# A planner without floors under the latest times of its early pieces

## The chip, the cores and the metric

The kernel runs on one core of a Trainium2 chip. The metric is the device time of one execution in microseconds (us). A core has TensorE (PE in the profile, with its weight loads as PEld), VectorE (DVE), ScalarE (ACT), GpSimd (POOL), and DMA queues; this kernel issues all its transfers from SyncE (SP).

## What is computed

An attention between two sets of rows, in both directions, gives 2304 tokens of 512 numbers (4 batches of 512 and of 32 rows); two MLPs follow, one behind the other. Everything is float32.

```python
# x: 4 x 8 x 512 x 64, state: 4 x 8 x 32 x 64
a  = softmax(x @ state.T / 8);   xread = a @ state
a2 = softmax(state @ x.T / 8);   sread = a2 @ x
x  = concatenate([xread, sread])           # as 2304 tokens x 512

h = x @ w_in                               # 512 -> 2048
x = (h * tanh(softplus(h))) @ w_out        # 2048 -> 512

xn = x / rms(x) * rms_g
g, val = xn @ w_gate, xn @ w_val           # 512 -> 1536
out = (g * sigmoid(g) * val) @ w_out2      # 1536 -> 512
```

## The kernel before

**Precision.** A matmul of the MLPs is made of three f16 matmuls: each operand is a high and a low f16 part, scaled by a power of two. The parts have to be made on the chip. Inputs arrive as 64-bit floats in this kernel, so a block of weights goes through a chain of steps: a load of two halves of 1 MB each into a staging region (L543), the rebuilding of a 32-bit float from its words (high words L470 or L468, sign L562, low word L567 or L569, joined at L578), a sum of squares (L599 on ACT) that a matmul with ones adds over the partitions (L481 on PE), a power-of-two scale from it (L489 to L497 on DVE, products of scales at L507), and then the split: the high part (L468 on ACT or L472 on DVE) and the low part (L612, DVE only).

**Pieces.** `attention(b)` is the attention of batch b: loads of x (L709), transposes on PE (L714, L723), scores (L737), the softmax over 32 columns on DVE and ACT (L777 to L800), PE's reads of state (L755) with the high part (L468) and the low part (L763) of the result written into the tile `slot` of the batch, and the second direction (`second`, L803 to L838). The state is loaded once, at L674. `plain(w, u)` loads and splits block u of the first MLP's weights; `wi` is w_in, `wo` is w_out, four blocks each. `group(gi, c, us, ...)` is the first MLP for batch c and the weight blocks us: pieces of 12 matmuls of 128x512 in the first layer (L918), the activation on ACT (L929), its high part (L468) and its low part g (L933, DVE), and pieces of 6 matmuls in the second layer (L955), summed in PSUM and copied out at the end of a group (L972). `keep(w, u, k, after)` prepares a block of the second MLP's weights (`wg` gate, `wv` value, `w2` out) in one of two staging regions (`psm` for k = 0, `attm` for k = 1), forms the sums of a product scheme with seven instead of eight block products, splits them, and stores the result to DRAM (L1367, `kept_...`), from where it is loaded again when the second MLP (`gated`) needs it.

**Who sets the order.** No line of the kernel gives the order of the engines' instructions. Each of these pieces registers steps with `op()`: what a step costs on each engine that could do it, what it reads and writes, and for PE's main matmuls a wanted time `at`. The class `Plan` then makes a plan for all engines. `chains()` goes back from the wanted and due times and gives each step a latest time: the steps of DVE and ACT behind it are counted at 5.5 times their cost (`SPARE`). `forward()` walks through time and, whenever an engine is free, gives it the ready step with the smallest latest time (a step that DVE could leave to ACT counts 4 us later there). `backward()` derives new latest times from the plan that was found, and the next round goes forward with those. There are 10 rounds, and the plan with the earliest end is kept. The instructions are then issued in that order, and on the chip semaphores hold each one until its inputs are there. The planner's times are a model; what runs together on the chip is decided by the semaphores.

**Floors.** `op()` also notes a floor, when one is set:

```python
o.floor = None if self.floor is None else self.floor()       # L72
...
if o.floor is not None:                                      # L156, in chains()
    late[o] = max(late[o], o.floor)
```

A step with a floor does not get a latest time below it from its chain of needs; it is then taken later than its chain alone would have it, and steps without a floor go first. Floors enter only into the latest times of the first round; the later rounds start from the plan of that round. T0, the wanted time of the first piece of the first MLP, is 22. Before the change attention 1 and wo block 0 have a floor of 12 (T0 - 10), the blocks 1, 2 and 3 of wi and wo have 22, 62 and 102, attention 2 has 102 and attention 3 has 142. Attention 0 and wi block 0 have none. The prepared blocks of `keep` (122 and more, 222 and more) and the steps of `gated` have floors of their own.

Of the kernel before, what the change touches and what calls it, by code (L numbers as in the profile page):

```python
# [318 lines left out]
def attn_moe_moe_kernel(  # L319
# [23 lines left out]
    P = Plan(nc)  # L343
# [271 lines left out]
    def plain(w, u, m, at, xexp, pool="raw", after=()):  # L615

        def dst(k):
            return m(at + 256 + 512 * k, 512).rearrange("p (a f) -> p a f", a=2)

        def dn(k):  # L620
            return m.names(at + 256 + 512 * k, 512)

        fetch(w, u, dst, dn, pool, after)
        s = norms([(m(at + 256 + 1024 * i, 1024).rearrange("p (a n) -> p a n", a=2), [*dn(2 * i), *dn(2 * i + 1)])
                   for i in range(2)], (w, u), xexp, f"{w}{u}", 2)
        for k in range(4):
            split(m, at, k, s, ((w, u), "s"), f"{w}{u}")
# [314 lines left out]
    def flush():  # L942
        if pending:
            l2(*pending.pop(0))
# [453 lines left out]
    with tc.manual_schedule():  # L1398
# [7 lines left out]
        state_scale()  # L1406
        attention(0)
        plain("wi", 0, *home["wi", 0], XEXP)
        P.floor = lambda: T0 + -10
        attention(1)  # L1410
        P.floor = lambda: T0 + -10
        plain("wo", 0, *home["wo", 0], XEXP)
        P.floor = None
        for u in range(1, U1):
            P.floor = (lambda v: lambda: T0 + v)([0, 40, 80][u - 1])
            plain("wi", u, *home["wi", u], XEXP)
            plain("wo", u, *home["wo", u], XEXP)
        P.floor = None
        bar = op({"X": 0.01}, lambda e: None, w=["early"], after=list(early_raw), name="early")
        every = list(range(U1))  # L1420
        group(0, 0, [0], None, 2)
# [2 lines left out]
        group(3, 1, [1], 3, 3)  # L1424
        group(4, 0, [2, 3], 2, 0)
        flush()
        P.floor = lambda: T0 + 80
        attention(2, clock[0] + DUE2)
        P.floor = None
        group(5, 1, [2, 3], 3, 1)  # L1430
        flush()
        P.floor = lambda: T0 + 120
        attention(3, clock[0] + DUE3)
        P.floor = None
        sread_scale(clock[0] + DUE3)
        done = op({"X": 0.01}, lambda e: None, r=held, after=list(att_ops), name="release")
        for w, u, k in (("wg", 0, 0), ("wv", 0, 0), ("wg", 1, 0), ("wv", 1, 1), ("wg", 2, 0), ("wv", 2, 1),
# [24 lines left out]
T0 = 22.0  # L1462
# [33 lines left out]
```

## Time and profile before

| | before |
|---|---|
| median of 3 runs | 799.59 us (795.63 to 801.95) |
| the profiled execution, its own time | 798.37 us |
| its span | 796.6 us |
| PE busy | 767.1 us (96%) |
| PEld (weight loads) busy | 523.8 us (66%) |
| DVE busy | 634.7 us (80%) |
| ACT busy | 445.2 us (56%) |
| mean granted clock of PE, of full speed | 0.977 |

The span runs from the first to the last recorded instruction of the profiled execution; its own time is 1.8 us longer. Times inside the span count from its start. The granted clock reads 1.00 at 2.4 GHz and 0.50 at 1.2 GHz. A line such as L918 is the line of the kernel that issued the instruction, and "out<-in" are the names of the tiles, so `slot<-a,page,slot` reads a PSUM bank `a`, a scalar in a `page` and the tile `slot`, and writes `slot`. `p` and `a` are PSUM banks, `w` and `w2m` hold the first MLP's weights, `psm` and `attm` are staging regions, `tt` is scratch, `g` holds split activations. "[3.17 <-ACT junk L599]" is idle time of the engine just before the instruction, and the instruction whose end released it.

### The profile page before, as it was taken

Reading aid. Unit: us, or ns where it says so; the run is one execution under the profiler, and the core shown is the slowest. Engines: PE = TensorE matmul, PEld = TensorE weight load, DVE = VectorE, ACT = ScalarE, POOL = GpSimd, SP = SyncE. Lnnn points to the kernel's source line nnn. Section 1 sums busy time; section 2 is a strip of 40 time slices with the busy share of each in tenths; the row PEclk is TensorE's granted clock in tenths of the full one; section 3 lists DMA queues with packets and bytes.
Section 4 is the critical chain, followed back from the end, with each engine's and each line's share of the span. In section 5 each row is a group of like instructions: output and inputs, shape, how many; then the busy total and the mean of one; then the engine's idle time right before and its main releaser. Section 6 shows DMA issues by size and latency. Waiting matters only on the chain.

```text
span 796.6 us, 14334 instructions
## 1 busy us (share of the span) xinstructions
PE 767.1 (96%) x5882; PEld 523.8 (66%) x5882; DVE 634.7 (80%) x1303; ACT 445.2 (56%) x812; POOL 0.7 (0%) x6
## 2 busy tenths in 40 slices
PE   6699999999999989999999999999999999999997
PEld 4344444444444434774457778888888889999996
DVE  3999999997997788899589679758984999566560
ACT  4999997666857577867475353425530744123220
POOL 0000000000000000000000000000000000000000
PEclk9599999999999989999999999999999999999999
DMA  8554643205041734523545964357434745275001
GB/s 208 181 144 168 216 156 106 50 5 204 9 158 53 245 125 199 173 107 124 210 156 205 388 227 150 121 187 278 178 117 170 276 167 186 93 284 204 16 2 67
DMA packets 36950, 125.71 MB, mean 158 GB/s; under 512 B 20116, under 2 KB 20116, under 8 KB 30740
## 3 DMA queue, kind: packets, MB, share of 16 engines
q1 hardware_dynamic: 36884, 124.79, 44.1%
q8 instruction: 46, 0.75, 0.4%
q14 instruction: 20, 0.16, 0.1%
HBM read 101.45 MB, written 23.33 MB: 157 GB/s over the span
## 4 chain that ended last, share of the span: by engine, by line
PE 57%; DVE 26%; ACT 9%; DMA 5%; issue 2%; SPq 1%; DVEq 0%; ACTq 0%
PE p L1103 27%; PE a L1187 13%; PE a L955 7%; PE p L918 5%; DVE g L933 3%; DVE psm L612 2%; PE p L1263 2%; ACT junk L599 2%; DMA kept_wg<-psm 2%; DVE sxm L562 2%; ACT sxm L567 1%; DVE w2m L612 1%; DVE page L507 1%; DMA kept_wv<-attm 1%; ACT psm L468 1%
## 5 line engine op out<-in xcount | busy, mean ns | idle before, releaser
L918 PE MATMUL p<-slot,w 128*128 128x512 f16 (+1 forms) x960 | 189.6, 353 | 0.4 <-ACT tt L468 0.4
L955 PE MATMUL a<-g,w2m 128*128 128x512 f16 (+1 forms) x960 | 187.2, 347 | 0.0
L918 PEld LDWEIGHTS <-w 128*128 128x128 f16 x960 | 87.3, 100 | 92.5 <-issue 6.8
L955 PEld LDWEIGHTS <-w2m 128*128 128x128 f16 x960 | 85.7, 99 | 88.3 <-issue 4.6
L1103 PEld LDWEIGHTS <-w 128*128 128x128 f16 x1344 | 131.4, 98 | 17.5 <-issue 0.3
L1115 DVE TENSOR_TENSOR tt<-p,tt 128x512 f32<-128x512 f32 x120 | 82.2, 686 | 43.8 <-PE p L1103 43.1
L1103 PE MATMUL p<-slot,w 128*128 128x256 f16 x768 | 92.6, 273 | 0.0
L1103 PEld LDWEIGHTS <-attm 128*128 128x128 f16 x672 | 65.7, 98 | 9.5 <-issue 1.0
L1187 PE MATMUL a<-attm,w2m 128*128 128x256 f16 x576 | 65.7, 273 | 0.0
L1187 PEld LDWEIGHTS <-w2m 128*128 128x128 f16 x576 | 56.3, 98 | 6.5
L468 ACT ACTIVATE w2m<-tt 128x512 f16<-128x512 f32 x42 | 25.0, 622 | 61.2 <-DVE tt L1154 47.6
L933 DVE SCALAR_TENSOR_TENSOR g<-tt,page,g 128x512 f16<-128x512 f32 x68 | 50.4, 747 | 3.0 <-ACT g L468 2.1
L929 ACT ACTIVATE tt<-p,page 128x512 f32<-128x512 f32 x68 | 45.6, 674 | 12.2 <-PE p L918 12.1
L1187 PE MATMUL a<-psm,g 128*128 128x256 f16 x432 | 51.6, 273 | 0.0
L468 ACT ACTIVATE psm<-psm,page 128x512 f16<-128x512 f32 (+1 forms) x42 | 30.0, 719 | 33.4 <-DVE psm L612 27.3
L1103 PE MATMUL p<-slot,attm 128*128 128x256 f16 x384 | 45.7, 273 | 0.2 <-DVE tt L1115 0.2
L1187 PEld LDWEIGHTS <-g 128*128 128x128 f16 x432 | 42.2, 98 | 5.4 <-issue 0.6
L468 ACT ACTIVATE g<-tt 128x512 f16<-128x512 f32 x30 | 18.2, 624 | 45.5 <-DVE tt L1154 23.4
L1139 ACT ACTIVATE tt<-tt,page 128x512 f32<-128x512 f32 x36 | 25.8, 720 | 31.6 <-DVE tt L1115 31.5
L567 ACT ACTIVATE sxm<-psm 128x512 uint16<-128x512 uint16 x46 | 35.2, 777 | 2.6 <-DMA psm<-in_moe_w_gate_dram 2.3
L1146 DVE TENSOR_TENSOR w2m<-tt,w2m 128x512 f16<-128x512 f32 x48 | 32.1, 683 | 2.0 <-ACT w2m L468 1.7
L468 ACT ACTIVATE slot<-a,page 128x512 f32<-128x512 f32 (+2 forms) x25 | 16.2, 655 | 30.2 <-PE a L1301 11.1
(197 smaller groups left out, 1078.1 us busy)
## 6 DMA issues: line engine op xcount, KB each, us to landing
w<-kept_wg SPq DMA_DIRECT2D x8, 1792.0 KB, 7.2
w<-kept_wv SPq DMA_DIRECT2D x8, 1792.0 KB, 8.1
attm<-kept_w SPq DMA_DIRECT2D x12, 1024.0 KB, 7.5
psm<-in_moe_w_out_dram SPq DMA_DIRECT2D x10, 1024.0 KB, 5.0
psm<-in_moe_w_in_dram SPq DMA_DIRECT2D x8, 1024.0 KB, 5.1
attm<-kept_wg SPq DMA_DIRECT2D x4, 1792.0 KB, 7.3
attm<-kept_wv SPq DMA_DIRECT2D x4, 1792.0 KB, 7.3
psm<-in_moe_w_gate_dram SPq DMA_DIRECT2D x6, 1024.0 KB, 5.1
```

Source lines behind the costliest of these rows:

```text
L468: nc.scalar.activation(o, i, ACTF.Copy, scale=1.0 if scale is None else scale)
L567: nc.scalar.activation(s16[:, :, 0], r16[:, :, 1], ACTF.Copy, scale=2.0 ** -13, bias=2.0 ** -14 - 0.5)
L612: op({"V": v1(512)}, lambda e: nc.vector.scalar_tensor_tensor(lo, f, s, h, ALU.mult, ALU.subtract), r=[*fn_, *hn, sname], w=ln, name=f"sl ...
L918: nc.tensor.matmul(P[ph][:, i * n:(i + 1) * n], part("wi", u, k, a)[:, f * 128:(f + 1) * 128], xh[:, k, b, :], start=m == 0, stop=m == 3 * ...
L929: op({"A": a_ps(512) + 0.09}, lambda e, s=s, ph=ph, ce=ce: nc.scalar.activation(P[s], P[ph], ACTF.Mish, scale=ce), r=[ph, f"ce{c}_{u}"], w ...
L933: op({"V": v1(512) + 0.06}, lambda e, s=s, g=g, u=u: nc.vector.scalar_tensor_tensor(P[g][:, 1, :], P[s], rho[u], P[g][:, 0, :], ALU.mult, ...
L955: nc.tensor.matmul(P[ya[d]][:, :n], part("wo", u, f, a)[:, d * 128:(d + 1) * 128], P[g][:, b, i * n:(i + 1) * n], start=first and m == 0, ...
L1103: nc.tensor.matmul(P[to][:, f * 256:f * 256 + 256], part(w, u, j, a)[:, k * 256 + f * 128:k * 256 + f * 128 + 128], h[:, k, b, :], start=b ...
L1115: op({"V": v1(512) + 0.06}, lambda e: nc.vector.tensor_tensor(P[to], P[bank_], P[a], ALU.add), r=[bank_, a], w=[to], name=f"{w} add")
L1139: op({"A": a_ps(512) + 0.09}, lambda e, i=i, o=o: nc.scalar.activation(P[o], P[i], ACTF.Silu, scale=c3), r=[i, f"c3{u}"], w=[o], tab="silu ...
L1146: op({"V": v1(512)}, lambda e: nc.vector.tensor_tensor(P[g][:, 1, :], P[s], P[g][:, 0, :], ALU.subtract), r=[s], w=[g], name="gl")
L1187: nc.tensor.matmul(P[to][:, t * 256:t * 256 + 256], P[g][:, a, o:o + 128], part("w2", u, j, b)[:, f * 256:f * 256 + 256], start=begin and ...
```

## The change

The floors of the early pieces go: those of attention 1, of wo block 0, of the blocks 1 to 3 of wi and wo, and of attention 2 and 3. Their steps get latest times from their chains alone. The floors of `keep` and `gated` stay. No step is added or taken away, and no cost or wanted time is changed. The whole diff:

```diff
--- before.py
+++ after.py
@@ -1406,16 +1406,11 @@
         state_scale()
         attention(0)
         plain("wi", 0, *home["wi", 0], XEXP)
-        P.floor = lambda: T0 + -10
         attention(1)
-        P.floor = lambda: T0 + -10
         plain("wo", 0, *home["wo", 0], XEXP)
-        P.floor = None
         for u in range(1, U1):
-            P.floor = (lambda v: lambda: T0 + v)([0, 40, 80][u - 1])
             plain("wi", u, *home["wi", u], XEXP)
             plain("wo", u, *home["wo", u], XEXP)
-        P.floor = None
         bar = op({"X": 0.01}, lambda e: None, w=["early"], after=list(early_raw), name="early")
         every = list(range(U1))
         group(0, 0, [0], None, 2)
@@ -1424,14 +1419,10 @@
         group(3, 1, [1], 3, 3)
         group(4, 0, [2, 3], 2, 0)
         flush()
-        P.floor = lambda: T0 + 80
         attention(2, clock[0] + DUE2)
-        P.floor = None
         group(5, 1, [2, 3], 3, 1)
         flush()
-        P.floor = lambda: T0 + 120
         attention(3, clock[0] + DUE3)
-        P.floor = None
         sread_scale(clock[0] + DUE3)
         done = op({"X": 0.01}, lambda e: None, r=held, after=list(att_ops), name="release")
         for w, u, k in (("wg", 0, 0), ("wv", 0, 0), ("wg", 1, 0), ("wv", 1, 1), ("wg", 2, 0), ("wv", 2, 1),
```

What the planner makes of it shows in the order of the engines. Three places follow.

DVE, at the end of the split of the first weight block (`w1_69`), first as it stands in the kernel before. `slot0_76` is the tile of batch 0, `p0_83` holds scores of batch 1:

```order
L578 SCALAR_TENSOR_TENSOR w2m_70<-w2m_70,sxm_74 128x512
L612 SCALAR_TENSOR_TENSOR w1_69<-w1_69,page1_100 128x512
L763 SCALAR_TENSOR_TENSOR slot0_76<-a0_87,page0_68,slot0_76 128x512
L763 SCALAR_TENSOR_TENSOR slot0_76<-a1_88,page0_68,slot0_76 128x512
L777 STREAM_TRANSPOSE attm_71<-p0_83 128x512
L780 TENSOR_REDUCE page1_100<-p0_83 128x1
```

The low parts of batch 0's last reads (L763) come right behind the last split row (L612), and batch 1's softmax (L777 on) begins behind them. DVE at the same place after the change:

```order
L798 TENSOR_TENSOR attm_71<-attm_71,page2_101 128x512 x2
L470 COPY tt_73<-p1_84 128x512
L763 SCALAR_TENSOR_TENSOR slot0_76<-a0_87,page0_68,slot0_76 128x512
L763 SCALAR_TENSOR_TENSOR slot0_76<-a1_88,page0_68,slot0_76 128x512
L800 STREAM_TRANSPOSE tt_73<-attm_71 128x512 x2
L612 SCALAR_TENSOR_TENSOR w1_69<-w1_69,page1_100 128x512
```

Batch 1's softmax up to its last step (L800) now stands ahead of the last split row, which moved from row 61 to row 87 of DVE's order. Two more rows of batch 0 and 1, L803 and L804, still stand behind it.

PE, just ahead of the first matmul of the first MLP (L918), in the kernel before. `p0_83` and `p2_85` take the scores of batch 1:

```order
L737 MATMUL p0_83<-tt_73,attm_71 32x512
L737 MATMUL p2_85<-tt_73,attm_71 32x512
L714 MATMUL p3_86<-ident_66,attm_71 128x128
L918 LDWEIGHTS w1_69
L918 MATMUL p1_84<-slot0_76,w1_69 128x512
```

The scores of batch 1 and the transpose of batch 2's state (L714) come first, then the MLP. The same place after the change:

```order
L714 MATMUL p2_85<-ident_66,attm_71 128x128
L723 MATMUL p3_86<-ident_66,attm_71 128x128 x4
L481 MATMUL p2_85<-page2_101,ones_67 128x2
L755 MATMUL a0_87<-tt_73,attm_71 64x512 x2
L755 MATMUL a1_88<-tt_73,attm_71 64x512 x2
L723 MATMUL p1_84<-ident_66,attm_71 128x128 x4
L723 MATMUL p0_83<-ident_66,attm_71 128x128 x4
L723 MATMUL p3_86<-ident_66,attm_71 128x128 x4
L755 MATMUL a0_87<-tt_73,attm_71 64x512 x2
L755 MATMUL a1_88<-tt_73,attm_71 64x512 x2
L918 LDWEIGHTS w1_69
L918 MATMUL p2_85<-slot0_76,w1_69 128x512
```

Batch 1's reads (L755) and batch 2's transposes (L723) moved ahead of the first matmul of the MLP.

SP, whose queue issues the transfers, where the second MLP's blocks pass through the staging regions, in the kernel before. `psm_72` takes gate blocks (and out block 1), `attm_71` the value blocks 1 and 2:

```order
L1367 DMA kept_wg1_108<-psm_72 128x4096
L543 DMA attm_71<-in_moe2_w_val_dram 128x2x1024
L543 DMA psm_72<-in_moe2_w_gate_dram 128x2x1024
L543 DMA attm_71<-in_moe2_w_val_dram 128x2x1024
L543 DMA psm_72<-in_moe2_w_out_dram 128x2x1024
L543 DMA attm_71<-in_moe2_w_val_dram 128x2x1024
L1367 DMA kept_wv1_110<-attm_71 128x4096
L1367 DMA kept_wg2_111<-psm_72 128x4096
```

The same place after the change:

```order
L1367 DMA kept_wg1_108<-psm_72 128x4096
L543 DMA psm_72<-in_moe2_w_gate_dram 128x2x1024
L543 DMA attm_71<-in_moe2_w_val_dram 128x2x1024
L543 DMA psm_72<-in_moe2_w_out_dram 128x2x1024
L543 DMA attm_71<-in_moe2_w_val_dram 128x2x1024 x2
L1367 DMA kept_wg2_111<-psm_72 128x4096
L1367 DMA kept_wv1_110<-attm_71 128x4096
```

The second half of gate block 2 is now issued ahead of the first half of value block 1, and gate 2's store ahead of value 1's. At the start of the queue, the order before is seven state pieces, the first half of the first weight block, four x pieces, one state piece, four x pieces, the second half; after the change it is four x, two state, four x and six state pieces, and only then the two halves of the weight block.

Further along, DVE's last split row of the first gate block moves from row 399 of its order to row 421, and that of the first value block from 486 to 489; all of DVE's order has 1168 rows before and 1146 after, since equal rows that stand together are printed as one and some conversions move to ACT. ACT's order has 22 table loads before and 24 after.

## Rows read from the trace of the kernel before

**Rows 1.** The page, busy time, share of the span and instructions by engine.

```profile
PE 767.1 (96%) x5882; PEld 523.8 (66%) x5882; DVE 634.7 (80%) x1303; ACT 445.2 (56%) x812; POOL 0.7 (0%) x6
```

**Rows 2.** Stretches: us, length, busy PE PEld DVE ACT POOL, clock, DMA share, GB/s.

```profile
30.00:40.00 10.00, 6.60 (x65) 2.36 (x55) 9.56 (x19) 9.06 (x18) 0.00 (x0) 0.50 0.38 121
100.00:150.00 50.00, 50.00 (x253) 23.46 (x252) 48.58 (x140) 43.72 (x82) 0.00 (x0) 1.00 0.31 103
150.00:200.00 50.00, 48.37 (x307) 23.08 (x305) 43.38 (x115) 30.00 (x48) 0.00 (x0) 1.00 0.32 106
250.00:300.00 50.00, 46.83 (x217) 20.52 (x215) 40.14 (x86) 31.77 (x69) 0.00 (x0) 0.93 0.42 147
```

**Rows 3.** Timeline of DVE, front: start us, us, instructions, [idle before <-releaser].

```profile
9.26 0.80 DVE L562 TENSOR_SCALAR sxm<-psm 128x512 uint16<-128x512 uint16 x2 [8.26 <-DMA psm<-in_moe_w_in_dram]
...
16.07 0.69 DVE L470 COPY tt<-p 128x512 f32<-128x512 f32 x1 [3.13 <-PE p L723]
...
39.74 0.74 DVE L612 SCALAR_TENSOR_TENSOR w<-w,page 128x512 f16<-128x512 f32 x1
40.84 1.41 DVE L763 SCALAR_TENSOR_TENSOR slot<-a,page,slot 128x512 f16<-128x512 f32 x2 [0.35 <-ACT slot L468]
42.47 0.72 DVE L777 STREAM_TRANSPOSE attm<-p 128x512 f32<-128x512 f32 x1 [0.22 <-PE p L737]
...
52.97 1.30 DVE L800 STREAM_TRANSPOSE tt<-attm 128x512 f32<-128x512 f32 x2
```

**Rows 4.** Timeline of PE, front.

```profile
16.08 1.79 PE L737 MATMUL p<-tt,attm 64*32 64x512 f32 x16
...
42.58 3.06 PE L918 MATMUL p<-slot,w 128*128 128x512 f16 x12
...
63.74 4.41 PE L918 MATMUL p<-slot,w 128*128 128x512 f16 x12
...
81.73 5.34 PE L918 MATMUL p<-slot,w 128*128 128x512 f16 x24
86.91 2.75 PE L955 MATMUL a<-g,w2m 128*128 128x512 f16 x12
```

**Rows 5.** Timeline of the DMA queue, first transfers.

```profile
0.73 3.24 SPq L674 DMA_DIRECT2D attm<-in_state_dram  x7
...
4.49 2.67 SPq L709 DMA_DIRECT2D attm<-in_x_dram  x4
```

**Rows 6.** Waits of PE, 100 to 340: waiting <- releaser: us, count, longest.

```profile
PE p L723 <- DVE attm L470: 0.7, 1, 0.7
PE p L834 <- DVE attm L470: 0.6, 2, 0.4
PE p L815 <- DVE attm L472: 0.6, 1, 0.6
```

**Rows 7.** Timeline of the DMA queue, stores of the first two gate blocks.

```profile
178.47 0.36 SPq L1367 DMA_DIRECT2D kept_wg<-psm  x1
...
262.59 0.34 SPq L1367 DMA_DIRECT2D kept_wg<-psm  x1
```

**Rows 8.** Timeline of DVE, behind the first of these stores.

```profile
184.88 0.43 DVE L472 TENSOR_SCALAR psm<-psm 128x512 f32<-128x512 f32 x1 [2.81 <-DMA kept_wg<-psm]
```

**Rows 9.** Timeline of PE, sums of squares of the second MLP's blocks.

```profile
205.79 0.28 PE L481 MATMUL p<-page,ones 128*128 128x8 f32 x2
...
289.56 0.59 PE L481 MATMUL p<-page,ones 128*128 128x8 f32 x2 [3.17 <-ACT junk L599]
290.01 5.28 PE L918 MATMUL p<-slot,w 128*128 128x512 f16 x12
```

**Rows 10.** Chain of waits that ended last, 240 to 330: start us, us, step.

```profile
262.59 7.29 DMA kept_wg<-psm
```

**Rows 11.** Timeline of ACT, a table load and the next activation.

```profile
53.05 1.28 ACT L286 ACT_TABLE_LOAD   x1
54.39 1.85 ACT L929 ACTIVATE tt<-p,page 128x512 f32<-128x512 f32 x3
```

## The prediction

> **What bounds the kernel now.** I read the page first, then busy time by stretch, then the PE timeline around the two stretches where PE stands still, then the DVE, ACT and DMA-queue rows that end those waits. The page gives PE 767.1 us of a 796.6 us span [rows 1]: only 29.5 us are not PE's, so whatever this change does to the order, it can win little and lose more. The stretches say where those 29.5 us lie. Between 30 and 40 us PE is busy 6.60 of 10 at a granted clock of 0.50 (the 1.2 GHz level), while DVE and ACT are full; from 100 to 150 PE is busy throughout and DVE 48.58 of 50; from 150 to 200 DVE falls to 43.38; from 250 to 300 PE loses 3.2 us and its clock reads 0.93 [rows 2]. So the front is bound by DVE and ACT, the rest by PE, and DVE has no room to spare before 150 us.
>
> In the front PE waits for two things. The first weight block must be split (last split row on DVE at 39.74) and block 0 of the activations must have its low halves (DVE to 42.25) [rows 3]; the first L918 starts right then, at 42.58 [rows 4]. After that PE is held again by batch 1's attention: the piece of 12 matmuls at 63.74 takes 4.41 us where 12 take 2.59 at full clock (24 from 81.73 to 86.91) [rows 4].
>
> **The change, term by term.** The profiled execution took 798.4 us, of which the span is 796.6; the median of the runs is 799.6. The sum is made against 798.4.
>
> *Start of group 0.* In the new order the softmax rows of batch 1 stand ahead of the last split of the first weight block on DVE, and batch 1's reads (L755) ahead of the first L918 on PE. In the kernel before those softmax rows run behind the split, from 42.47 to 54.27 without a hole [rows 3]: 11.8 us, less 0.3 for L803 and L804, which stay behind. One copy joins them (L470, 0.7 with its like at 16.07), three rows of about 0.6 go to ACT: net +10.5. The start of DVE's work moves too. The queue now issues the eight x pieces (4 in 2.67, so 5.3) and eight state pieces (7 in 3.24, so 3.7) before any weight [rows 5], done at 0.73 + 9.0 = 9.7; with the transposes behind them the score matmuls end near 14.7 instead of 17.9 [rows 4]. But what DVE does before its first L777 at 18.2 now, from 9.26 to 11.9 and from 16.07 on [rows 3], 4.8 us in all, comes after: 4.8 less the 3.2 won is 1.6 late. So DVE is done at 42.25 + 10.5 + 1.6 = 54.4, and with the reads between (1.1 at full clock, 2.0 at half) the first L918 starts near 56, 13.4 us later than now.
>
> Most of this comes back, since PE no longer waits for batch 1 afterwards. From 42.58 to 86.91, where the second layer of group 1 starts, PE takes 44.3 us [rows 4]. Its work there is 8 first-layer pieces of 2.59, 8 second-layer pieces of 1.29 and some 6.9 of attention matmuls: 38.0. Batch 1's first reads and batch 2's transposes, 3.2 us, are already done in the new order: 34.8, and 1.3 for a first piece at the 1.2 GHz level. 56 + 34.8 + 1.3 = 92.1 against 86.91: **+5.2**. Bounds: +2 if DVE's start is won back in full, +9 if ACT, which has to deliver the same splits, paces it 4 us slower.
>
> *Small waits.* PE's four short waits for attention copies, 0.7 + 0.6 + 0.6 [rows 6], arise where batches 2 and 3 are threaded through groups 4 and 5. Both batches now come earlier; PE, running 5 us later against DVE, finds the copies made: **-1.9**, between -1.9 and 0.
>
> *The store chain.* The second MLP's weights pass one by one through one staging region: split, stored, and only then is the next converted. With the attention ahead of it, the last split of the first gate block moves from DVE row 399 to 421. Ahead of it 28 attention operations come in and 7 go out, the rest cancels: 21 at about 0.6 each [rows 3], 13 us more DVE work; with DVE 1.6 late besides, the store goes out at 178.47 + 14.6 = 193 [rows 7] instead, and lands 7 later, at 200. The next DVE row in line overwrites the region, and DVE's queue stands behind it, as it does now for 2.81 us at 184.88 [rows 8]. Queued behind it are the L933 rows that group 5's second layer waits for: 8 us of DVE work, so 208, against PE's arrival at about 206. And PE's L481 for the value block, at 205.79 now without a wait [rows 9], needs its squares: from DVE's restart to that L481 the chain takes 21 us now, with batch 3's softmax among it; I take 17 without, so 217, against PE at 215. Two holds of 2 us: **+3.5**. Below: 0, if PE is later than I think. Above: 8, if the chain from landing to L481 takes the 21 us that it takes now.
>
> *The long wait.* PE now stands 3.17 us at L481 at 289.56, and the piece behind it takes 5.28 for its 12 matmuls [rows 9] where 12 such take 2.75 [rows 4]: 5.7 together. The squares it needs come from value block 1, whose chain starts when the store at 262.59 has landed, 7.29 later [rows 7, 10]. In the new order the gate block 2 goes first through that gap (its load stands ahead of value block 1's on the queue), and the L481 at this place in PE's order is gate 2's. Its splits are not crowded by batch 3's softmax any more: the stretch from the first gate store to the last value split was 87 DVE rows and is now 68. Relative to PE the store at 262.59 comes about 5 us sooner, so PE, later by its 7, finds both sums ready: **-5.7**; 0 if the wait stays.
>
> *Table loads.* ACT's order has 24 table loads instead of 22, the two more among batches 2 and 3. A load takes 1.28 us and the next activation follows at once, 53.05 to 54.39 [rows 11]: 2.6 us on an engine that is 30.00 of 50 busy in 150 to 200 [rows 2], so 0 on the path; 2.6 if ACT paced it. The Trainium skill (ScalarE: Activation LUTs, What ACT_TABLE_LOAD costs) puts a switch at 2.66 us with a drain of 1.38 behind the load, which would make it 5.3. The rows here show no such drain; by either figure it lies beside other work.
>
> Nothing else changes in kind: same matmuls, same bytes, same stores; the loads behind 330 us stand in nearly the same order.
>
> **Sum:** 798.4 + 5.2 - 1.9 + 3.5 - 5.7 = 799.5. The profiled run lies 1.2 under the median, so for a median I say 800.7, rounded to 801.
>
> **The rivals.**
> *The long wait stays.* Value 1's load now stands behind gate 2's on the queue, so its first half is issued some 7 us later after the store; if the chain has no room, PE waits there as before. For it: the chain is serial and its DMA time fixed. Against it: PE itself is later. Then 805.2.
> *DVE becomes the bound (slower).* Batches 2 and 3 move into the stretch where DVE has 1.4 us free in 50 [rows 2]. Place: the L933 rows before the second-layer pieces of groups 2 to 4. Ahead of group 4's last piece stand 11 us more DVE work; PE has 5.6 us more work ahead and starts 5.2 later, which just cancels. So there is no slack, and from the point where DVE and ACT lose more than about 1 us to each other, every further us is paid. At a pace 7% worse over the 130 us, 9 more, it ends near 809 to 812, more still if PE's pauses bring the 1.2 GHz level back as at 290.01. For it: at several pieces of groups 2 to 4 the two sums lie within 1 us of each other. Against: eleven conversions and copies move from DVE to ACT.
> *The front gets dense for nothing (faster).* If DVE works the reordered front without the small holes that it has now, and the first L918 starts by 50, the first term is -1; with no store hold and the long wait gone: 798.4 - 1 - 1.9 - 5.7 = 790. The Trainium skill (Perfetto Trace Analysis, Optimization Strategy) says that a kernel whose bound changes over time may gain by interleaving those regimes, which is what this order does more of. By that rule the time is nearer this end; here the regime that takes the extra work is already full on DVE.
> *It changes nothing that counts.* All shifts lie beside other work, and the long wait only moves: 798 to 800.
>
> **How the numbers follow.** Forecast (late start paid back): 0.40, its own range 797 to 805. Long wait stays: 0.22, 803 to 809. DVE bound: 0.18, 808 to 816. Dense front: 0.08, 787 to 793. Nothing: 0.12. About 1% is what a measurement can tell from no change here, 8 us: faster is below 791.6, slower above 807.6. Faster: most of the dense front, 0.07. Slower: 0.17 of the DVE case, 0.06 of the long wait, 0.02 of the forecast's tail: 0.25. The same: 0.68. The range cuts the top of the DVE case and the bottom of the dense front: 792 to 812, which leaves about 0.17 out.
>
> **What would show it.** First L918 near 56 us (50 would speak for the dense front, 60 for ACT as the pace); the second layer of group 1 (L955) near 92. PE without waits over 1 us from there to about 190; waits of PE for L933 rows there would be the DVE case. The first kept_wg store near 193, DVE standing at the L472 row behind its landing, and PE held about 2 us by L933 or L481 between 200 and 220. No wait over 1 us at the L481 near 290 to 300, and no piece of 5 us behind it. The forecast is wrong above all if the late start is not paid back, or if the wait near 290 comes back in another place.

## The result and the profile after

The changed kernel takes 804.38 us (median of 10 runs, 801.95 to 805.54), the kernel before 800.95 us (median of 10 runs, 795.63 to 804.15). The ratio is 1.0052, with a 95% interval of 1.0033 to 1.0071: about 4 us slower, less than the 1% below which the prediction counts a time as the same. The forecast was 801 us and "the same". The profiled execution has a span of 802.7 us and an own time of 804.52 us; both are 6.1 us more than in the kernel before.

The page's busy time by engine, as in [rows 1]:

```profile
PE 765.7 (95%) x5882; PEld 523.3 (65%) x5882; DVE 630.3 (79%) x1292; ACT 455.4 (57%) x825; POOL 0.7 (0%) x6
```

Eleven DVE operations moved to ACT. PE's busy time is 1.4 us less on a span that is 6.1 us longer, so it stands idle 7.5 us more. The stretches of [rows 2] after the change (us, length, busy PE PEld DVE ACT POOL, clock, DMA share, GB/s):

```profile
30.00:40.00 10.00, 7.19 (x63) 2.53 (x63) 8.98 (x23) 9.04 (x17) 0.00 (x0) 0.50 0.67 195
100.00:150.00 50.00, 47.70 (x298) 23.21 (x297) 46.70 (x127) 46.65 (x74) 0.00 (x0) 0.97 0.31 90
150.00:200.00 50.00, 50.00 (x301) 24.28 (x300) 46.02 (x151) 32.20 (x60) 0.00 (x0) 1.00 0.17 64
250.00:300.00 50.00, 48.54 (x239) 21.61 (x236) 39.56 (x82) 34.44 (x74) 0.00 (x0) 1.00 0.41 148
```

From 100 to 150 PE was busy throughout; now it stands 2.3 us there. From 250 to 300 it now loses 1.5 us instead of 3.2. PE's timeline at the places that the prediction named:

```profile
54.95 7.04 PE L918 MATMUL p<-slot,w 128*128 128x512 f16 x24
...
91.77 2.75 PE L955 MATMUL a<-g,w2m 128*128 128x512 f16 x12
...
126.59 1.23 PE L723 MATMUL p<-ident,attm 128*128 128x128 f32 x8 [0.17 <-DMA attm<-in_x_dram]
128.06 0.33 PE L714 MATMUL p<-ident,attm 128*128 128x128 f32 x1 [0.24 <-ACT tt L929]
130.28 1.03 PE L723 MATMUL p<-ident,attm 128*128 128x128 f32 x4 [1.89 <-ACT tt L929]
131.11 2.77 PE L955 MATMUL a<-g,w2m 128*128 128x512 f16 x6
...
216.55 0.39 PE L481 MATMUL p<-page,ones 128*128 128x8 f32 x2 [1.47 <-ACT junk L599]
...
294.34 0.30 PE L481 MATMUL p<-page,ones 128*128 128x8 f32 x2
...
300.30 0.39 PE L481 MATMUL p<-page,ones 128*128 128x8 f32 x2 [1.76 <-ACT junk L599]
300.54 5.73 PE L955 MATMUL a<-g,w2m 128*128 128x512 f16 x18
```

The first L918 starts at 54.95 instead of 42.58, the second layer of group 1 at 91.77 instead of 86.91 [rows 4]. A hold at 126 to 131 us is new; the 6 matmuls behind it take 2.77 us where 6 take 1.46 in the same trace (the row at 297.08, not shown). The long wait at L481 [rows 9] is half of what it was: gate block 2's sum at 294.34 waits for nothing, value block 1's at 300.30 waits 1.76 us, and the 18 matmuls behind it take 5.73 where 24 take 5.34.

The DMA queue around the two gate stores, as in [rows 7], and DVE behind the first of them, as in [rows 8]:

```profile
194.07 0.35 SPq L1367 DMA_DIRECT2D kept_wg<-psm  x1
...
265.87 0.34 SPq L1367 DMA_DIRECT2D kept_wg<-psm  x1
274.08 0.37 SPq L543 DMA_DIRECT2D psm<-in_moe_w_gate_dram  x1
274.54 0.43 SPq L543 DMA_DIRECT2D attm<-in_moe_w_val_dram  x1
```

```profile
201.03 0.43 DVE L472 TENSOR_SCALAR psm<-psm 128x512 f32<-128x512 f32 x1 [3.73 <-DMA kept_wg<-psm]
```

To see where the 6.1 us come from I add up, stretch by stretch, what PE loses: its idle time (the stretch less its busy time), and half of its busy time where the granted clock was 0.50.

| stretch, us | before: idle + slow clock | after: idle + slow clock | after less before |
|---|---|---|---|
| 0 to 60 | 17.2 + 8.8 | 24.7 + 10.2 | +8.8 |
| 60 to 100 | 1.0 + 1.7 | 0.1 + 0 | -2.6 |
| 100 to 210 | 2.0 + 0 | 2.3 + 1.7 | +2.0 |
| 210 to 285 | 0 | 1.5 + 0 | +1.5 |
| 285 to 310 | 3.2 + 3.1 | 1.8 + 1.7 | -2.8 |
| 310 to the end | 6.2 + 0 | 6.8 + 0 | +0.6 |
| sum | 43.2 | 50.6 | +7.4 |

The sum is 1.3 us more than the difference of the spans, since the ends of matmuls are modelled; a term is good to about 1 us. This count is called PE's loss below. It says where PE lost time, not why.

### The profile page after: what moved, and what is told of

It reads as the page before. It is cut to its first block, busy times and chain, and to the rows that moved or that the text cites. A ratio compares the mean times of both kernels' runs of the same rounds, so it can differ in the third digit from the quotient of the medians.

```text
span 802.7 us, 14343 instructions
## 1 busy us (share of the span) xinstructions
PE 765.7 (95%) x5882; PEld 523.3 (65%) x5882; DVE 630.3 (79%) x1292; ACT 455.4 (57%) x825; POOL 0.7 (0%) x6
## 4 chain that ended last, share of the span: by engine, by line
PE 64%; DVE 18%; ACT 10%; DMA 4%; issue 2%; SPq 1%; DVEq 0%; ACTq 0%
PE p L1103 26%; PE a L1187 13%; PE a L955 11%; PE p L918 9%; ACT junk L599 2%; PE p L1263 2%; DVE g L933 2%; DMA attm<-in_moe_w_val_dram 2%; DVE sxm L562 1%; ACT sxm L567 1%; ACT L286 1%; DMA w<-kept_wg 1%; ACT attm L468 1%; PE a L1301 1%; ACT tt L929 1%
## 5 line engine op out<-in xcount | busy, mean ns | idle before, releaser
L955 PE MATMUL a<-g,w2m 128*128 128x512 f16 (+1 forms) x960 | 189.4, 351 | 0.1
L918 PE MATMUL p<-slot,w 128*128 128x512 f16 (+1 forms) x960 | 186.1, 349 | 0.0
L955 PEld LDWEIGHTS <-w2m 128*128 128x128 f16 x960 | 86.4, 99 | 91.2 <-issue 7.4
L918 PEld LDWEIGHTS <-w 128*128 128x128 f16 x960 | 86.0, 99 | 91.6 <-issue 4.6
L929 ACT ACTIVATE tt<-p,page 128x512 f32<-128x512 f32 x68 | 45.9, 676 | 19.2 <-PE p L918 19.0
L933 DVE SCALAR_TENSOR_TENSOR g<-tt,page,g 128x512 f16<-128x512 f32 x68 | 50.3, 747 | 5.3 <-ACT g L468 4.6
L1139 ACT ACTIVATE tt<-tt,page 128x512 f32<-128x512 f32 x36 | 25.9, 720 | 36.9 <-DVE tt L1115 36.7
L468 ACT ACTIVATE g<-tt 128x512 f16<-128x512 f32 x33 | 19.8, 623 | 43.8 <-DVE tt L1154 22.3
L468 ACT ACTIVATE tt<-p 128x512 f32<-128x512 f32 x32 | 18.7, 592 | 33.3 <-PE p L1103 24.1
L468 ACT ACTIVATE attm<-attm,page 128x512 f16<-128x512 f32 (+1 forms) x38 | 27.1, 719 | 15.4 <-DVE attm L612 12.9
L612 DVE SCALAR_TENSOR_TENSOR psm<-psm,page 128x512 f16<-128x512 f32 x40 | 29.9, 748 | 4.3 <-ACT psm L468 3.4
```

The source lines that it names most:

```text
L468: nc.scalar.activation(o, i, ACTF.Copy, scale=1.0 if scale is None else scale)
L612: op({"V": v1(512)}, lambda e: nc.vector.scalar_tensor_tensor(lo, f, s, h, ALU.mult, ALU.subtract), r=[*fn_, *hn, sname], w=ln, name=f"sl ...
L918: nc.tensor.matmul(P[ph][:, i * n:(i + 1) * n], part("wi", u, k, a)[:, f * 128:(f + 1) * 128], xh[:, k, b, :], start=m == 0, stop=m == 3 * ...
L929: op({"A": a_ps(512) + 0.09}, lambda e, s=s, ph=ph, ce=ce: nc.scalar.activation(P[s], P[ph], ACTF.Mish, scale=ce), r=[ph, f"ce{c}_{u}"], w ...
L933: op({"V": v1(512) + 0.06}, lambda e, s=s, g=g, u=u: nc.vector.scalar_tensor_tensor(P[g][:, 1, :], P[s], rho[u], P[g][:, 0, :], ALU.mult, ...
L955: nc.tensor.matmul(P[ya[d]][:, :n], part("wo", u, f, a)[:, d * 128:(d + 1) * 128], P[g][:, b, i * n:(i + 1) * n], start=first and m == 0, ...
```

## The experiments

Two theories went into the runs. **A: PE's losses add**, so each term of the prediction can be taken away alone. **B: near 290 us PE meets the chain of the second MLP's weights** (store, load, conversion, squares), which runs at its own pace; what PE wins or loses ahead of that point only changes how long it waits there.

### The floors by groups

The floors fall into three groups: front (attention 1 and wo block 0), blocks (blocks 1 to 3 of wi and wo) and late (attention 2 and 3). Six kernels complete the table of all eight combinations. Relative to the changed kernel, `f_w` puts the blocks' floors back:

```diff
         for u in range(1, U1):
+            P.floor = (lambda v: lambda: T0 + v)([0, 40, 80][u - 1])
             plain("wi", u, *home["wi", u], XEXP)
             plain("wo", u, *home["wo", u], XEXP)
+        P.floor = None
```

> Only the blocks 1 to 3 of wi and wo have their floors back. Theory: the front and batch 3's place stay as in the changed kernel, so first L918 near 55 us and the hold near 126 us of about 4 us; queue order value 1 first, long wait back to about 6 us if the queue order sets it: span 803 to 805.5. Rival (the hold comes from conversions of these blocks on ACT): no hold at 126 us, span 799 to 801.

`f_23` puts the late ones back:

```diff
+        P.floor = lambda: T0 + 80
         attention(2, clock[0] + DUE2)
+        P.floor = None
...
+        P.floor = lambda: T0 + 120
         attention(3, clock[0] + DUE3)
+        P.floor = None
```

> Attention 2 and attention 3 have their floors back. Theory: batches 2 and 3 run where they ran before, so the hold at 126 us is gone (-4.0) and their short waits are back (up to +2.0); first L918 stays near 55 us (+4.9 against before is paid); the first gate store goes out earlier than 194 us, so that the L481 near 216 us waits for nothing (-1.5). Queue order value 1 first: long wait back to about 6 us (+2.8). Span about 802. Rival (PE being later is what shortened the long wait): span about 799.

`f_front` puts the front ones back:

```diff
+        P.floor = lambda: T0 + -10
         attention(1)
         plain("wo", 0, *home["wo", 0], XEXP)
+        P.floor = None
```

> Only attention 1 and wo block 0 have their floors back. If the weight blocks' floors are what counts: slower than before, ratio 1.003 to 1.010, with the last store of gate block 1 later than 265 us. If the front's own floors were the ones that counted: first L918 near 45 us and ratio 0.996 to 1.000.

`f_fw` has the first and the third of these edits, which leaves only the late floors out.

> All floors back but those of attention 2 and 3; the order of PE, DVE and ACT up to the second layer of group 1 is that of the kernel before, and batches 2 and 3 stand early as with the floors of the weight blocks alone (span 796.0 there). Theory A (PE's losses add): first L918 back near 43 us and about 5 to 6 us less lost by 100 us than with the weight blocks' floors alone, so a span near 790. Theory B (near 290 us PE meets the chain of value block 1, which runs at its own pace; what PE has won ahead of that it waits there): the 5 us come back as a wait at L481 near 285 to 295 us, as in the kernel before, span 795 to 798.

`f_w23` has the first and the second, which leaves only the front floors out.

> All floors back but those of attention 1 and wo block 0: only the front is that of the changed kernel, with the first L918 near 55 us. Theory A (losses add): 5 to 6 us more lost by 100 us than in the kernel before and nothing given back, so a ratio to before of about 1.006. Theory B (the long wait near 290 us takes up what PE is late): the wait there shrinks from 6.3 us of idle and slow clock to 1 or less, ratio 0.999 to 1.002.

`f_f23` has the second and the third, which leaves only the blocks' floors out.

> All floors back but those of the weight blocks 1 to 3. The order of PE's front is that of the changed kernel all the same (batch 1's reads ahead of the first L918, near 55 us), batches 2 and 3 stand where they stood before. If the weight blocks' floors are what the change loses by (every kernel so far without them is slower than before, every one with them is not): ratio 1.003 to 1.008. If the late first L918 alone cost nothing and the early batches 2 and 3 were the loss: ratio 1.000.

What was measured (loss by 285 us and time of gate block 1's store from each profile):

| floors kept | kernel | ratio to before, interval | first L918, us | PE's loss by 285 us | store of gate 1, us |
|---|---|---|---|---|---|
| all | before | 1 | 42.58 | 30.8 | 262.59 |
| front, blocks | f_fw | 0.9961 (0.9938 to 0.9985) | 42.20 | 33.3 | 263.00 |
| blocks, late | f_w23 | 0.9987 (0.9972 to 1.0003) | 55.86 | 37.6 | 268.59 |
| blocks | f_w | 0.9996 (0.9982 to 1.0010) | 54.56 | 36.7 | 263.84 |
| front, late | f_f23 | 1.0043 (1.0029 to 1.0057) | 57.90 | 43.8 | 273.77 |
| front | f_front | 1.0023 (1.0010 to 1.0037) | 46.38 | 39.8 | 268.72 |
| late | f_23 | 1.0062 (1.0043 to 1.0082) | 54.59 | 40.7 | 269.59 |
| none | after | 1.0052 (1.0033 to 1.0071) | 54.95 | 40.4 | 265.87 |

Three things follow. Every kernel without the blocks' floors is slower than the kernel before, none with them is: taking them out costs 0.43 to 0.75% in all four pairs of the table. Four pairs of one planner's orders are few, since the other two groups, too, move the time by up to 0.39%; what speaks against chance is that all four have one sign, and that none of the other groups' eight shifts in the table is as large (`f_a1`, further down, differs from the changed kernel by 0.57%, with one floor put back). Whether another way of holding these blocks back would do the same was not tried. The front's floors cost between -0.13 and 0.35% when they go, though the first L918 then starts 8 to 13 us later in three of the four pairs. The late ones matter between -0.39 and +0.09%: taking them out alone is a gain, and `f_fw` at 0.9961 beats both kernels.

Against their expectations: `f_f23` came out as the blocks' floors had it (1.0043 in 1.003 to 1.008), with a first L918 later than expected (57.90, not 55). `f_front` at 1.0023 is below its 1.003 to 1.010, but the rival (1.000 or less) is out. `f_w23` fits theory B: ratio 0.9987, and the wait near 290 us is gone. `f_fw` fits neither: its span is 794.2, and the time won in the front (28.6 us of loss by 100 us, 35.3 in `f_w`) is in part lost again before 285 us, in short holds near 125 us and one of 2.17 us at 212 to 214, not at the L481 near 290.

The expectation for `f_w` was that the hold near 126 us and the late front stay, at a span of 803 to 805.5 us. The front did (54.56), the rest did not: the span is 796.0 us, the median time 799.02. Its waits of PE (waiting, releaser, us, count, longest) from 100 to 340 us:

```profile
PE p L826 <- ACT attm L468: 0.8, 1, 0.8
PE p L723 <- ACT tt L929: 0.7, 1, 0.7
PE p L481 <- ACT junk L599: 0.3, 1, 0.3
```

That is all: 1.8 us, and the clock stays at 1.00 there, against 5.5 us in the changed kernel. The rival written for that run, that the conversions of these blocks make the hold, has the hold right; its span of 799 to 801 is still above the measured one. `f_23` was expected at a span near 802 and its profile has 801.9 (median time 804.53), but not by the terms expected: batches 2 and 3 stand where they stood before, the hold is gone from 126 us, and 3.7 us of waits appear at 144 to 154 instead; the wait near 290, expected back at 6 us, is 2.4. So the hold isn't tied to batch 3. In `f_f23` it is at 156:

```profile
PE p L815 <- DVE attm L472: 2.4, 1, 2.4
PE p L723 <- ACT tt L929: 1.5, 1, 1.5
PE p L481 <- ACT junk L599: 0.5, 1, 0.5
PE p L834 <- DVE attm L470: 0.2, 1, 0.2
```

Between 100 and 180 us the eight profiles without the blocks' floors (all runs of this study) lose 2.3 to 4.6 us of PE, 3.6 on average; the six with them 0 to 3.0, 1.3 on average; the two sets overlap. `f_front` shows that the front's place isn't the cause of this: its first L918 starts at 46.38, and it loses 2.9 us there all the same.

### Single floors

`f_3` puts back the floor of attention 3 alone, `f_a1` that of attention 1 alone (the lines of the diffs above).

> Only attention 3 has its floor back. Theory (the losses add, place by place: late start of group 0 +4.9 us, PE held at batch 3's transposes between 126 and 134 us +4.0, short waits of batches 2 and 3 -2.0, sum of squares at 216 us +1.5, long wait near 290 to 300 us -2.8): batch 3's transposes return to about 190 us, so no idle PE and no 1.2 GHz between 125 and 140 us, -4.0; first L918 stays near 55 us. The queue issues value block 1 ahead of gate block 2 again, as in the kernel before; if that order sets the long wait, it is back at about 6 us (idle and slow clock), +2.8, and the span is about 801.5. Rival 1 (the hold comes from ACT, crowded with conversions of the weight blocks 2 and 3, not from batch 3): the hold stays, span 803 or more. Rival 2 (the long wait shrank because PE is later, not because of the queue): it stays at about 3.5, span about 799.

> Only attention 1 has its floor back. Theory: the first L918 is back near 43 us and the second layer of group 1 (L955) near 87 us, -4.9; the hold at batch 3's transposes near 126 us stays at about 4 us, since its order on PE is that of the changed kernel; the queue keeps gate 2 ahead of value 1, so the long wait stays near 3.5 us. Span about 798, less what DVE loses at 100 to 130 us with PE 5 us earlier. Rival (the late start is paid back later anyway because DVE is the bound up to 130 us): PE waits 3 to 5 us more in 90 to 140 us and the span stays at 802 to 803.

`f_3`: 801.09 us, ratio 1.0021 (1.0007 to 1.0035), span 800.4. Batch 3's transposes are back at 195 us, and the hold is still there, at 133 to 135, now behind ACT's exponentials of batch 2 and an L972 row of DVE (3.7 us with the slow clock). The span is near the expected 801.5 for the wrong reason: the hold stayed, and the long wait is 0.5 us, not 6, although the queue issues value block 1 first, so that order doesn't bring the wait back. `f_a1`: 808.02 us, ratio 1.0109 (1.0088 to 1.0129), the slowest of all; its span is 805.9, where 798 was expected. Its floor doesn't bring the old front back: the first L918 starts at 48.61, PE loses 2.9 us between 60 and 100, 1.5 to 125 and 1.6 at batch 3's transposes, and 4.26 at L481 at 219.91. A floor on one piece reorders all the others; it doesn't undo one term.

### One step moved in the changed kernel

In `m_tr` and `m_q` the plan of the changed kernel is kept, and a few steps are moved before the instructions are issued. `m_tr` holds batch 3's transposes and scores back until group 2's last piece is out:

```diff
+    held, waits, out, behind = [], set(), [], "l2 g2 p1 d3"
+    for t, o, e in plan:
+        if behind and (o.name == "att3" and e == "T" or o.deps & waits):
+            held.append((t, o, e))
+            waits.add(o)
+            continue
+        out.append((t, o, e))
+        if o.name == behind:
+            out += held
+            behind = None
```

> The changed kernel with one thing moved: batch 3's transposes and scores on PE, and what needs them, stand behind the second-layer matmuls of group 2's last piece instead of ahead of and between them. Theory (PE's own order makes the hold: the transposes wait for PSUM banks that ACT's L929 has to empty, while second-layer matmuls whose inputs are ready stand behind them): the 2.3 us of idle PE and the 1.7 us of slow clock between 126 and 134 us vanish, nothing takes their place, span about 799 against 802.7. Rival (DVE and ACT are behind at this point whatever PE does first): PE waits 2 to 4 us a little later, for L933, L972 or copies of batch 3, span within 1.5 us of 802.7.

803.81 us, ratio 1.0041 (1.0024 to 1.0057), span 802.7: the rival. At the transposes 0.9 us are left, and PE waits elsewhere instead. From 100 to 180 us:

```profile
PE p L918 <- ACT tt L929: 1.5, 1, 1.5
PE p L723 <- ACT tt L468: 0.9, 1, 0.9
PE p L826 <- ACT attm L468: 0.2, 1, 0.2
```

All three are ACT's. In the changed kernel ACT has no gap from 98.17 us to the L929 at 129.57 that releases PE at 130.28. A part of its timeline there:

```profile
101.69 1.28 ACT L286 ACT_TABLE_LOAD   x1
...
104.45 1.28 ACT L286 ACT_TABLE_LOAD   x1
105.75 0.69 ACT L929 ACTIVATE tt<-p,page 128x512 f32<-128x512 f32 x1
106.46 1.28 ACT L286 ACT_TABLE_LOAD   x1
107.75 0.63 ACT L789 ACTIVATE attm<-attm 128x512 f32<-128x512 f32 x1
108.40 1.28 ACT L286 ACT_TABLE_LOAD   x1
109.69 0.69 ACT L929 ACTIVATE tt<-p,page 128x512 f32<-128x512 f32 x1
110.40 1.28 ACT L286 ACT_TABLE_LOAD   x1
```

With a sixth at 114.11 that is 7.7 us of table loads in 14, because batch 2's softmax alternates with L929 just where ACT is full; in the kernel before ACT loads no table between 60 and 140 us. From 100 to 120 us ACT is equally full there, but from 120 to 130 it is 7.32 of 10 busy, in the changed kernel 10.00. `f_w` has four loads there. That the loads alone make the hold isn't shown: `f_fw` has six too (97 to 110 us) and loses 2.5 us between 100 and 180. An order with the exponentials grouped was not tried.

`m_q` moves one transfer:

```diff
+    k = [o.name for _, o, _ in plan]
+    a, b = k.index("load wg21"), k.index("load wv10")
+    return plan[:a] + [plan[b]] + plan[a:b] + plan[b + 1:]
```

> The changed kernel with one thing moved: on the DMA queue the first half of value block 1 is issued ahead of the second half of gate block 2, as in the kernel before. Theory (the order on the queue makes the rest of the long wait): the value load goes out as soon as batch 3's last reads have left its region, about 273 us instead of 274.5, and lands alone in 5 to 6 us instead of 8.6, so value 1's sums of squares are ready 3 to 5 us earlier; the wait at L481 near 300 us (1.8 idle, 1.7 slow clock) goes, span about 799.5. Rival 1 (gate block 2's L481 near 294 us, whose load now lands later, waits in its place): span as before the move, 802 to 803. Rival 2 (the wait comes from ACT's squares, not from the load): wait at 300 us unchanged, same span.

802.04 us, ratio 1.0018 (1.0000 to 1.0036), so about 2.7 us less than the changed kernel by the two ratios; their intervals overlap by a little. The load goes out 5.3 us after the store (269.09) instead of 8.7, the wait at value block 1's L481 is 0.63 us, and no slow clock follows:

```profile
296.98 0.39 PE L481 MATMUL p<-page,ones 128*128 128x8 f32 x2 [0.63 <-ACT junk L599]
```

The 2.8 us that left this place are about what the time won. So in the changed kernel's order the place of this load makes most of the wait. It is not the only thing that does: the kernel before, `f_23` and `f_3` all issue value block 1 first, and wait 3.17, 2.37 and 0.51 us.

### Where PE meets the chain

`b_pad` is the kernel before with matmuls that nobody needs:

```diff
-                    for r in range(2):
+                    for r in [0, 1] * (4 if (b, g) == (3, 0) else 1):
                         nc.tensor.matmul(
```

> The kernel before, with the first half of batch 3's reads (L755 near 224 us) computed four times instead of once: 24 matmuls, 3.3 us more work for PE, in the same place of the same order, with the same result. Theory B (near 290 us PE meets value block 1's chain, which runs at its own pace, and waits 3.17 us for it; the wait is followed by 6.9 us at 1.2 GHz, which cost 3.1 us more): the added work fills the wait, the clock does not fall, and the kernel with more work is not slower but up to 3 us faster, ratio to before 0.996 to 1.000, L481 still near 289.6 us. Theory A (PE's work and losses add up to the span): 3.3 us slower, ratio 1.004.

799.51 us, ratio 1.0002 (0.9982 to 1.0021). The matmuls stand at 261.71, not 224, and cost 6.1 us there instead of 3.3 (7.19 where these reads took 1.11), since the clock fell under them. PE's timeline in the kernel before:

```profile
261.86 1.11 PE L755 MATMUL p<-tt,attm 32*64 32x512 f32 x16
...
283.63 2.75 PE L918 MATMUL p<-slot,w 128*128 128x512 f16 x12
...
296.72 0.28 PE L481 MATMUL p<-page,ones 128*128 128x8 f32 x2
```

and with the padding:

```profile
261.71 7.19 PE L755 MATMUL p<-tt,attm 32*64 32x512 f32 x40
268.83 4.34 PE L955 MATMUL a<-g,w2m 128*128 128x512 f16 x12
...
291.14 2.75 PE L918 MATMUL p<-slot,w 128*128 128x512 f16 x12
293.73 0.29 PE L481 MATMUL p<-page,ones 128*128 128x8 f32 x2
293.88 2.75 PE L918 MATMUL p<-slot,w 128*128 128x512 f16 x12
296.46 1.46 PE L955 MATMUL a<-g,w2m 128*128 128x512 f16 x6
297.76 0.28 PE L481 MATMUL p<-page,ones 128*128 128x8 f32 x2
```

The 12 first-layer matmuls ahead of the sum start 7.5 us later than in the kernel before (291.14 against 283.63). There L481 waited 3.17 us and the next 12 matmuls took 5.28 [rows 9]; here it waits for nothing and they take 2.75. By the second L481 the padded kernel is 1.0 us behind (297.76 against 296.72), and over all runs there is no difference (the profiled execution alone has a span of 799.0, 2.4 us longer). Theory A would have made it 3 to 6 us slower, which the interval excludes. So the kernel before had about 6 us of PE's time to give away ahead of 290 us: some 3 in that wait, and some 3 in the slow clock behind it, which didn't come.

That the chain runs at its own pace is not what this run shows, though: L481 was expected to stay near 289.6 and came at 293.73. The last squares of value block 1 on ACT end at 289.5 in the kernel before and at 293.6 here, 4.1 us later, just ahead of PE. The padded matmuls are themselves an input of the chain: DVE waits for them, its first row behind the gate store starts at 272.37 instead of 269.91, and its first on value block 1 at 277.94 instead of 273.85. DVE's row behind the reads, before and padded:

```profile
263.04 0.75 DVE L472 TENSOR_SCALAR slot<-p,page 128x512 f16<-128x512 f32 x1 [0.48 <-PE p L755]
```

```profile
268.94 0.75 DVE L472 TENSOR_SCALAR slot<-p,page 128x512 f16<-128x512 f32 x1 [6.63 <-PE p L755]
```

The cleaner case for the chain is `f_fw`, without padding. Its gate store (263.00) and the end of these squares (289.6) come when those of the kernel before do, although PE starts the 12 matmuls ahead of the sum 3.2 us later (286.80). L481 then waits for nothing, and no slow clock follows, which is about the gain:

```profile
289.67 0.39 PE L481 MATMUL p<-page,ones 128*128 128x8 f32 x2
```

`m_best` takes `f_fw` and moves value block 0's sum (L481, held 2.17 us at 214) one first-layer piece later on PE, by the code of `m_tr` with that step and piece.

> The kernel with all floors but those of attention 2 and 3 (ratio to before 0.996), with the sum of squares of value block 0 (L481, held 2.17 us near 214 us) one first-layer piece of 12 matmuls later on PE. Theory A: PE finds the squares ready, 2.2 us less idle, ratio 0.9935. Theory B: PE reaches L481 near 290 us 2 us earlier and waits there for value block 1's chain, which is set by the stores and not by PE; same ratio as without the move, 0.995 to 0.998, or worse if the wait there gets long enough for the clock to fall.

797.17 us, ratio 0.9970 (0.9956 to 0.9985): no better than `f_fw`, the number of theory B. Its mechanism isn't shown: the hold is gone, but in the profile PE lost more in the front (32.2 us by 100 us against 28.6 in `f_fw`, in the same order) and came to the sum near 290 later, not earlier (292.6), so one profile can't show where the 2.2 us went.

## Why the prediction was right, and where its steps failed

The range held the time, and the case with most of the chance was its kind: the late start and the store chain cost, the long wait gives back, and all of it stays under 1%. Part of this is luck. The median of 804.38 lies as well in the range of the rival in which the long wait stays (803 to 809), and half of that rival happened; the forecast case's own range ends at 805. Two of the signs that were named beforehand failed: no wait over 1 us between 92 and 190 us (there is one of 1.89 at 128 to 130), and none at L481 near 290 to 300 (1.76). Against the profiled execution's own time the terms compare so:

| term | forecast | measured |
|---|---|---|
| late start of group 0, at group 1's second layer | +5.2 | +4.9 (91.77 against 86.91) |
| small waits | -1.9 | -2.0, and a new hold of +4.0 |
| store chain | +3.5 | +1.5 |
| long wait | -5.7 | -2.8 |
| table loads | 0 | on the path to the new hold |
| the rest | 0 | +0.6 |
| own time | 799.5 | 804.5 |

**Start of group 0.** Right step by step: score matmuls done at 13.6 (14.7 forecast), first L918 at 54.95 (56), L955 at 91.77 (92.1). One reading behind it was loose: the piece of 4.41 us at 63.74 in the kernel before isn't held by waits of its own; the clock was 0.50 from 63.7 to 67.1, behind waits of 1.38 and 0.46 us. But its price in the end is not 5 us. The front's floors alone are worth -0.13 to 0.35%, because the lateness is taken up by the long wait in `f_w23` and partly by shorter holds in `f_w`. Adding this term to the others in full was the error of method: it holds until the next point where PE waits for something else anyway (6.3 us of wait and slow clock near 290 in the kernel before, none in `f_w23`).

**Small waits.** The old ones went, as forecast. The step that failed is "PE, running 5 us later against DVE, finds the copies made": the rival of a full DVE and ACT is what happened, in a milder form, 4.0 us at 126 to 134. The place was another (batch 3's transposes, behind L929, not the L933 rows) and so was the engine: ACT, not DVE. The term **table loads** stands on the path to it. It was put at 0 because ACT is 30.00 of 50 busy from 150 to 200 us [rows 2]; batch 2's switches moved to 101 to 115 us, and ACT is 19.82 of 20 busy between 100 and 120. The cover was read from the stretch the loads came from, not the one they went to. How much of the 4.0 us is theirs wasn't separated. A load costs what [rows 11] show: 1.28 us at 104.45, and the next activation starts within 0.02 us of its end. The Trainium skill (ScalarE: Activation LUTs, What ACT_TABLE_LOAD costs) has a drain of 1.38 us behind a load; the trace after shows none either.

**Store chain.** The store was expected at 193 and went out at 194.07, DVE was expected to stand behind it and stood 3.73 us, and L481 was expected to be held 2 us at about 217 and was held 1.47 at 216.55. The hold at L933 didn't come.

**Long wait.** Half right. Gate block 2 went first, as said, and its sum was ready. The rival's mechanism was there too: value block 1's load was issued 8.7 us after the store instead of 0.6 (the forecast said some 7), and `m_q` shows that most of what was left of the wait came from this.

**What the prediction did not have.** It gave the blocks' floors no term ("nothing else changes in kind"), and they carry the loss: 0.43 to 0.75% over the pairs, 0.59 on average, where the whole result is 0.52. The late ones, whose absence the rival of a full DVE counts as a cost, are a small gain when they go. The Trainium skill (Perfetto Trace Analysis, Optimization Strategy) says that a kernel whose most contended engine changes over time may gain by interleaving its regimes, and batches 2 and 3 earlier among the groups are more of that. The four pairs agree weakly: 0.39, 0.20 and 0.10% faster, and 0.09% slower. What the blocks' floors do is partly open. Without them PE is held 2.3 to 4.6 us between 100 and 180 us, at other places in each order, and the store of gate block 1 goes out 2 to 11 us later in three of the four pairs and 1 us later in the fourth. Which rows of DVE or ACT carry that was not found: in two of the four pairs more conversion rows (L562, L569, L578) stand ahead of the sixteenth L933 on DVE, 8 and 7, in the other two fewer, 7 and 5.

## What to carry to other kernels

A late start is worth what the next meeting point leaves of it: look for the next place where the bounding engine waits for a chain of its own pace, and count only what passes that place. A wait that sits there can be tested by padding the bounding engine with work that nobody needs; if the time stays, gains ahead of it are likely worth little, and the clock behind the wait is what can be won. Put the padding where the chain doesn't wait for it: in `b_pad` it moved the chain as well. A rule in a planner is no term of a sum; try the rules alone and together (here eight kernels), since restoring one of them made the slowest kernel of all.

## What the runs showed of the hardware

**The clock fell under a busy PE.** In `b_pad` PE has no gap from 260 to 285 us, and yet the granted clock is 0.50 from 265.2 to 272.1. What it did before it fell was 3.5 us of the reads, float32 matmuls on tiles of 32 by 64. The stretches of `b_pad`, with columns as in [rows 2]:

```profile
260.00:285.00 25.00, 25.00 (x117) 9.80 (x115) 16.15 (x30) 11.98 (x20) 0.00 (x0) 0.86 0.63 218
285.00:300.00 15.00, 15.00 (x74) 7.03 (x72) 14.37 (x40) 13.36 (x42) 0.00 (x0) 1.00 0.36 128
```

**A hold of the same length brings the clock down or not.** The changed kernel and `m_q` have the same order up to 260 us and the same hold at batch 3's transposes, 2.3 us. Behind it the clock was 0.50 for 3.4 us in the first and stayed at 1.00 in the second:

```profile
125.00:140.00 15.00, 12.70 (x72) 6.34 (x71) 12.74 (x36) 12.47 (x24) 0.00 (x0) 0.89 0.40 107
```

```profile
125.00:140.00 15.00, 12.66 (x79) 6.31 (x78) 13.88 (x47) 14.15 (x27) 0.00 (x0) 1.00 0.38 101
```

A hold of 1.53 us in `m_tr` at 156 brought it down, one of 2.17 in `f_fw` at 214 did not. So the same wait has two prices here, and one profile shows only one of them.

**Orders that are the same lose differently.** Up to 100 us PE has one order in the changed kernel, `m_q` and `m_tr`, and PE's loss there is 34.9, 34.0 and 36.7 us. So a difference of less than 3 us can't be read from one profile of this kernel, and the small terms above are those of one execution each.
